# Batch 0's four head pairs merged in one written order on all engines

## The chip, the cores and the metric

One core of one Trainium2 chip runs the whole kernel as one program. The metric is device time in microseconds, as the median of several executions. The engines named here: TensorE (PE; its weight loads are listed as PEld), VectorE (DVE), ScalarE (ACT), GpSimd (POOL), and SyncE (SP), whose queue issues the DMA transfers.

## The reference

Attention in two parts, added, and a feed-forward layer on the result. The eight batches have eight heads, 576 positions and head dimension 64; the layer has 4608 tokens, width 512 and hidden width 2048.

```python
q_d, k_d, v_d = (mean over groups of 4 positions)      # 144 positions
out_up = np.repeat(softmax(scale * q_d @ k_d.T) @ v_d, 4, axis=2)
mask = np.abs(pos[:, None] - pos[None, :]) < 4         # a band of 7
out_local = softmax(where(mask, scale * q @ k.T, -1e9)) @ v
x = (out_up + out_local) as [batch * position, head * dim]
h = x @ w_in
out = (s * max(h, 0) ** 2 + b) @ w_out
```

## The kernel before, in words

**Units.** Attention is done for two heads at a time, a head pair (b, hp): 32 units. Units of batches 0 to 2 (`first_unit`) compute both parts on TensorE. The *far* part (`down`) sums q and k over four positions on VectorE (L276, L278), copies q into a block-diagonal tile on ScalarE (L282), sums v on GpSimd (L287 to L292), takes 3 score matmuls (`sa`, L303), the maximum (L304), three exponentials (L307), the normalisation (L311 to L314), transposes through TensorE (`tp`, `tr`, L322 to L327), copies them out (L329, L332) and multiplies with the summed v (`up`, L337, L339). The *near* part makes the banded scores from 24 small matmuls a head (`sl`, L388) on top of a mask matmul (L383), subtracts the maximum (L393, L394), takes the exponential (L397), normalises (L398 to L401, the last on GpSimd in batch 0), transposes in blocks of 32 on VectorE (L411), copies the blocks into a block-diagonal tile `bd` (L414) and multiplies with windows of v (`ol`, L431). L434 adds both parts into the tile x. Units of later batches do the near part on GpSimd and VectorE (`local_unit`).

**Rooms.** Unit (0,0) uses the standing tiles; units (0,1) to (0,3) borrow memory of weight tiles that are not filled yet (`make_room`), so that batch 0's units have no tile in common. Their block-diagonal tiles have to be zero first: `clear(i)` does that with GpSimd memsets (L187, L188). Unit (0,0)'s tiles `dq` and `db` are cleared by VectorE (L163, L174).

**Feed-forward.** Tokens go in 18 row blocks t of 256, the hidden width in 8 blocks p of 256. Each operand is split into a high and a low part and three products are taken: `gemm1(t, p)` (L556 to L558) into `ph`, activation on ScalarE (L566 to L568), low part on VectorE (`gl`, L569), `gemm2(t, p)` (L601 to L603). Weights arrive as 64-bit numbers and are rebuilt as 32-bit ones by `convert`: one ScalarE step (L226), four VectorE steps (L227 to L230), the high part on ScalarE (L231), the low part on VectorE (L234). Block p's raw words are staged in the memory of a later block's tile, `STAGE[p]`. `split_x(t)` splits the tokens (L542, L543).

**Order.** Row blocks 0 and 1 go through p = 0 to 6 together, then row block 2 does the same, then p = 7 for the three, then the others one by one. Weight block p is converted at a written step (`CONVERT_AT`), some with lowered priority (`BEHIND`). Batch 1 has to be complete before row block 2 starts. `advance` emits the steps of the attention units between the GEMMs at a written pace.

A scheduler reorders what the program emits: it keeps, for each engine, a list by priority (program order, moved by `high_priority`), and puts whichever instruction is ready first on the engine's queue by its own model of time. The queues are then fixed. Batch 0 is emitted unit by unit, with raised priority, so the scheduler decides how its units mix, and what else is put between:

```python
bk = banks(0, 1, 2, 3, 5, 6, 7)
for hp in range(HP):
    load_ahead(hp)
    if hp > 1:
        clear(hp)
    with tc.high_priority(offset=400):
        for _ in first_unit(0, hp, bk):
            pass
split_w(0)
```

PSUM has eight banks; batch 0's tiles take seven in turn, and bank 4 is left to the first `gemm1`.

Of the kernel before, what the change touches and what calls it, by code (L numbers as in the profile page):

```python
# [19 lines left out]
P = 128  # L20
# [29 lines left out]
STAGE = (6, 6, 7, 6, 7, 6, 7)  # L50
# [6 lines left out]
W_MAX = (1.875 - 2.0 ** -23) * 2.0 ** (31 - 127)  # L57

# [4 lines left out]
def attention_ffn_kernel(ctx, tc, qk, vw_in, vr_in, vdm, qkn, vn, w_in, w_out, s_in, b_in, out):  # L63
# [40 lines left out]
    def load_pair(b, hp):  # L104
        if (b, hp) in ld:
            return
        own = {}
        if b == 0 and hp:
            room[hp] = make_room(hp)
            own = room[hp]["load"]  # L110

        def load(tag, shape, src, pool=one):
            t = own[tag] if tag in own else pool.tile(shape, F32, tag=tag, name="t" + tag)
            nc.sync.dma_start(t, src)
            return t

        tqk = load("qk", [P, 2, SP], qk[b, hp], two)
        tvr = load("vr", [P, FAC, D], vr_in[b, hp])
        tvd = load("vd", [KM, FAC, P], vdm[b, hp])
        tvw = load("vw", [P, NG, P], vw_in[HP * b + hp]) if HP * b + hp < EU else None  # L120
        ld[(b, hp)] = (tqk, tvw, tvr, tvd)

    load_pair(0, 0)


    ident = cst.tile([P, P], F32, name="ident")
    make_identity(nc, ident)
    load_pair(0, 1)
# [25 lines left out]
    nc.gpsimd.memset(omask, 0.0)  # L154
    for u in range(2):
        mu = omask[64 * u : 64 * u + 64]
        keep(mu, [[1, CH], [1, NO]], -HALO, CH)
        keep(mu, [[-1, CH], [-1, NO]], S - 1 + HALO, -CH)

    dq = cst.tile([P, NQ * 2 * GQ + 3 * P], F32, name="dq")
    nc.vector.memset(dq, 0.0)  # L163
# [10 lines left out]
    nc.vector.memset(db, 0.0)  # L174
# [7 lines left out]

    def clear(i):
# [30 lines left out]
    def convert(st, hi, lo, op, p):  # L214
# [11 lines left out]
        nc.scalar.mul(f, top.bitcast(F32), 2.0 ** -112)  # L226
        nc.vector.tensor_scalar(f, f, W_MAX, -W_MAX, ALU.min, ALU.max)  # L227
        nc.vector.tensor_scalar(w, w, 3, 0x7FFFFFF8, ALU.logical_shift_left, ALU.bitwise_and)
        nc.vector.scalar_tensor_tensor(w, low, 29, w, ALU.logical_shift_right, ALU.bitwise_or)
        nc.vector.scalar_tensor_tensor(w, top, -0x80000000, w, ALU.bitwise_and, ALU.bitwise_or)  # L230
        nc.scalar.copy(hi, f)  # L231
        for i in range(0, n, 512):
# [3 lines left out]
    def split_w(p):  # L236
        with tc.high_priority(offset=-BEHIND.get(p, 0)):
            split_parts(p)

    def split_parts(p):  # L240
        wi[p] = one.tile([P, 2, NK, 256], F32R, tag=f"wi{p}", name="wi")
        wo[p] = one.tile([P, 2, 2, DM], F32R, tag=f"wo{p}", name="wo")
        for op, w in (("i", wi[p]), ("o", wo[p])):
            fl = w.rearrange("p s k f -> p s (k f)")
            if p < len(STAGE):
                st = wst.pop((p, op))
                for j in range(0, 1024, CHUNK[p]):
                    js = slice(j, j + CHUNK[p])
                    convert(st[:, js], fl[:, 0, js], fl[:, 1, js], op, p)
            else:  # L250
                for i in range(4):
                    cs = slice(256 * i, 256 * i + 256)
                    convert(load_quarter(p, op, i), fl[:, 0, cs], fl[:, 1, cs], op, p)
# [14 lines left out]
    def down(b, hp, banks, tmp, dg):  # L268

        _, qc, vdr, vm = dg  # L270
        tqk, _, tvr, tvd = ld[(b, hp)]
        qt, kt = tqk[:, 0], tqk[:, 1]

        qd = tmp([P, SD], "qd")
        kd = tmp([P, SD], "kd")
        nc.vector.tensor_reduce(  # L276
            qd, qt[:, 0:S].rearrange("p (s j) -> p s j", j=FAC), AX.X, ALU.add)
        nc.vector.tensor_reduce(  # L278
            kd, kt[:, 3 : 3 + S].rearrange("p (s j) -> p s j", j=FAC), AX.X, ALU.add)
        for h in range(2):  # L280
            hs = slice(64 * h, 64 * h + 64)
            nc.scalar.copy(  # L282
                qc[hs, :, GQ * h : GQ * h + GQ], qd[hs].rearrange("p (i s) -> p i s", i=NQ))
# [5 lines left out]
        for h in range(2):  # L289
            hs = slice(64 * h, 64 * h + 64)  # L290
            ve.tensor_tensor(vm[:, h, hs], vt[0:KM, 0, hs], vt[0:KM, 1, hs], ALU.add)
            ve.tensor_tensor(vdr[hs, hs], vq[hs, 0], vq[hs, 1], ALU.add)  # L292
        yield
# [7 lines left out]
        with first(b):  # L301
            for i in range(NQ):
                nc.tensor.matmul(sa[:, i], qc[:, i], kd, start=True, stop=True)  # L303
# [466 lines left out]
```

## Time and profile before

| | |
|---|---|
| median of 3 runs | 971.13 us (970.21 to 973.34) |
| span of the profiled execution | 970.7 us |
| TensorE busy | 938.7 us, 97% |
| VectorE busy | 637.7 us, 66% |
| ScalarE busy | 475.0 us, 49% |
| GpSimd busy | 418.0 us, 43% |
| DMA | 86.26 MB, mean 89 GB/s |

The profile is of one execution, and its span, 970.7 us, is 0.4 us under the median. Times in it are microseconds from the span's start. A row of the timeline gives start, duration, engine, line, operation, tiles and shapes, and in brackets how long the engine sat idle before and what ended that. A row of the groups gives, behind the bar, the busy time and the mean duration in ns, then the idle time before the group's instructions and its main releasers. Matmuls overlap and their ends are modelled, so their distances from start to start say more than their durations.

### The profile page before, as it was taken

The numbers are of one execution on the slowest core, as the hardware profiler recorded it, in microseconds if no ns is written. First come the engines' busy times: TensorE is split into PE (matmuls) and PEld (weight loads), VectorE is DVE, ScalarE is ACT, GpSimd is POOL, SyncE is SP. The second block draws the span as 40 slices with busy tenths as digits, with TensorE's granted clock in tenths as the row PEclk, the third lists the DMA queues.
The fourth block names the chain that finished last, engine by engine and source line by source line (L and its number), as shares of the span: only waits on it lengthen the run. The fifth ranks groups of instructions, "written<-read, shape, count | busy, mean of one in ns | idle before, by whom it ended". The sixth has DMA issues, their size and how long they took to land.

```text
span 970.7 us, 18541 instructions
## 1 busy us (share of the span) xinstructions
PE 938.7 (97%) x7316; PEld 843.4 (87%) x7316; DVE 637.7 (66%) x1175; ACT 475.0 (49%) x1141; POOL 418.0 (43%) x455
## 2 busy tenths in 40 slices
PE   5769999999999999999999999999999999999998
PEld 4559988888999999998888899989899999998987
DVE  5999996864567878787787878787878521211121
ACT  5878775553754453545363545453635433333231
POOL 9421011101066686776868786867676200000000
PEclk9999999999999999999999999999999999999999
DMA  9736512112243232323241424242412000000000
GB/s 316 261 121 210 172 60 78 49 42 73 101 134 113 77 110 72 102 70 133 67 136 66 135 68 131 72 134 69 136 55 76 1 22 1 23 1 22 1 23 22
DMA packets 32103, 86.26 MB, mean 89 GB/s; under 512 B 3344, under 2 KB 7952, under 8 KB 32016
## 3 DMA queue, kind: packets, MB, share of 16 engines
q1 hardware_dynamic: 32016, 85.08, 26.6%
q8 instruction: 57, 0.93, 0.4%
q14 instruction: 30, 0.25, 0.1%
HBM read 75.63 MB, written 9.44 MB: 88 GB/s over the span
## 4 chain that ended last, share of the span: by engine, by line
PE 74%; DVE 9%; DMA 8%; POOL 5%; ACT 2%; issue 2%; SPq 0%; DVEq 0%; ACTq 0%; POOLq 0%
PE ph L556 11%; PE ph L557 11%; PE ph L558 11%; PE po L603 11%; PE po L601 11%; PE po L602 11%; DMA tqk<-in_qk_dram 3%; POOL pr L466 3%; POOL acc L488 3%; DMA wst<-in_moe_w_out_dram 2%; PE sa L303 2%; DVE bias L579 1%; PE up L339 1%; PE ol L431 1%; DMA lqk<-in_qkn_dram 1%
## 5 line engine op out<-in xcount | busy, mean ns | idle before, releaser
L556 PE MATMUL ph<-xh,wi 128*128 128x256 f32 x1152 | 325.4, 283 | 3.7 <-ACT xh L542 2.5
L557 PE MATMUL ph<-xl,wi 128*128 128x256 f32 x1152 | 323.9, 281 | 0.0
L558 PE MATMUL ph<-xh,wi 128*128 128x256 f32 x1152 | 323.6, 281 | 0.0
L466 POOL TENSOR_TENSOR pr<-lqk 128x576 f32<-128x576 f32 x140 | 201.2, 1461 | 73.2 <-DMA lqk<-in_qkn_dram 29.2
L556 PEld LDWEIGHTS ph<-xh,wi 128*128 128x128 f32 x1152 | 217.5, 189 | 11.2 <-ACT xh L542 2.8
L557 PEld LDWEIGHTS ph<-xl,wi 128*128 128x128 f32 x1152 | 217.4, 189 | 5.4 <-issue 0.2
L558 PEld LDWEIGHTS ph<-xh,wi 128*128 128x128 f32 x1152 | 217.6, 189 | 0.3
L566 ACT ACTIVATE ph<-ph 128x512 f32<-128x512 f32 x144 | 83.8, 582 | 229.0 <-PE ph L558 223.2
L601 PE MATMUL po<-wo,gh 128*128 128x512 f32 x456 | 180.7, 396 | 0.0
L602 PE MATMUL po<-wo,gh 128*128 128x512 f32 x456 | 180.5, 396 | 0.0
L603 PE MATMUL po<-wo,gl 128*128 128x512 f32 x456 | 177.9, 397 | 0.0
L569 DVE TENSOR_TENSOR gl<-ph,gh 128x512 fp32r<-128x512 f32 x114 | 77.8, 683 | 115.8 <-ACT gh L568 115.5
L488 POOL TENSOR_TENSOR acc<-acc,pv 128x576 f32<-128x576 f32 x80 | 114.4, 1430 | 57.1 <-DVE acc L488 29.5
L468 DVE TENSOR_REDUCE st<-pr 128x9 f32<-128x576 f32 x140 | 105.9, 757 | 37.7 <-POOL pr L466 35.4
L292 POOL TENSOR_TENSOR dq<-vq 64x64 f32<-64x64 f32 x58 | 22.8, 393 | 197.4 <-PE up L337 195.3
L603 PEld LDWEIGHTS po<-wo,gl 128*128 128x128 f32 x456 | 85.7, 188 | 17.6 <-issue 0.2
L487 DVE TENSOR_TENSOR pv<-lv,st 128x576 f32<-128x576 f32 x120 | 87.5, 747 | 18.8 <-POOL acc L488 18.4
L601 PEld LDWEIGHTS po<-wo,gh 128*128 128x128 f32 x456 | 85.7, 188 | 15.9 <-ACT gh L568 0.6
L602 PEld LDWEIGHTS po<-wo,gh 128*128 128x128 f32 x456 | 85.7, 188 | 15.8
L568 ACT CAST gh<-ph 128x512 fp32r<-128x512 f32 x114 | 66.9, 587 | 64.3 <-PE po L602 62.4
L567 ACT ACTIVATE ph<-ph 128x512 f32<-128x512 f32 x144 | 83.7, 582 | 3.2
L602 PE MATMUL po<-wo,gb 128*128 128x512 f32 x120 | 47.1, 392 | 0.0
(149 smaller groups left out, 1239.3 us busy)
## 6 DMA issues: line engine op xcount, KB each, us to landing
tqk<-in_qk_dram SPq DMA_DIRECT2D x30, 584.0 KB, 4.1
lqk<-in_qkn_dram SPq DMA_DIRECT2D x20, 768.0 KB, 4.2
lv<-in_vn_dram SPq DMA_DIRECT2D x20, 480.0 KB, 3.4
out_dram<-os SPq DMA_DIRECT2D x17, 512.0 KB, 3.1
wst<-in_moe_w_in_dram SPq DMA_DIRECT2D x7, 1024.0 KB, 6.5
wst<-in_moe_w_out_dram SPq DMA_DIRECT2D x7, 1024.0 KB, 5.3
tvd<-in_vdm_dram SPq DMA_DIRECT2D x29, 160.0 KB, 2.9
tvr<-in_vr_dram SPq DMA_DIRECT2D x29, 128.0 KB, 3.1
```

Of the source, the lines that this page charges most:

```text
L466: nc.gpsimd.tensor_tensor(pr, lqk[:, 0:CH], lqk[:, CH + o : 2 * CH + o], ALU.mult)
L468: nc.vector.tensor_reduce(ls[:, :, o], pr, AX.X, ALU.add)
L487: nc.vector.tensor_tensor(pv, lv[:, o : o + CH], w, ALU.mult)
L488: (nc.vector if o % 3 == 1 else nc.gpsimd).tensor_tensor(acc[:, :, h], acc[:, :, h], pv, ALU.add)
L556: nc.tensor.matmul(ph[:, j], wi[p][:, 0, k, f], xh[:, k], start=(k == 0), stop=False)
L557: nc.tensor.matmul(ph[:, j], wi[p][:, 0, k, f], xl[:, k], start=False, stop=False)
L558: nc.tensor.matmul(ph[:, j], wi[p][:, 1, k, f], xh[:, k], start=False, stop=(k == NK - 1))
L566: nc.scalar.activation(ph, ph, AF.Relu)
L567: nc.scalar.activation(ph, ph, AF.Square)
L601: nc.tensor.matmul(po[m], gh[:, j, ms], wo[p][:, 0, j], start=first, stop=False)
L602: nc.tensor.matmul(po[m], gh[:, j, ms], wo[p][:, 1, j], start=False, stop=False)
L603: nc.tensor.matmul(po[m], gl[:, j, ms], wo[p][:, 0, j], start=False, stop=last)
```

## The change

Batch 0 is no longer emitted unit by unit. `first_unit` is taken apart into three step generators per unit: d (far part, 12 steps), l (near part, 13 steps) and v (value sums on GpSimd, one step). The conversion of weight block 0 becomes four more (c0 to c3, five steps each) and the split of row blocks 0 and 1 another (x, 8 steps; the first three pairs, then the fourth). A written string, `FRONT`, lists 132 steps in the order in which they are emitted, and `in_order` adds a dependency from each instruction to the one before it on its engine, so that the scheduler can't change this order. The first step of units (1,0) and (1,1) is chained behind it the same way.

The other edits: batch 0's PSUM tiles take all eight banks. The q/k tiles of the four pairs are loaded first, then all values, then the value windows of pair 0, weight block 0, and the windows of pairs 1 to 3; weight blocks 1 and 2 follow. Block 0 is staged in block 7's tiles instead of block 6's. Rooms 1 and 2 are cleared by ScalarE copies from a zero column, room 3 by VectorE memsets. The offset mask of the later batches is made after the front. Later units are emitted step by step as before.

```diff
-STAGE = (6, 6, 7, 6, 7, 6, 7)
+STAGE = (7, 6, 7, 6, 7, 6, 7)
...
+FRONT = (
+    "d0 l0 d0 d1 l1 d1 d0 d2 d1 d2 d0 l0 d0 v0 d2 d1 d0 d3 d1 l3 d2 v2 d1 d3 l1 l0 d2 d1 "
+    "l3 d0 l2 l0 d1 l3 d2 l2 l0 d0 l0 l2 d2 l0 c0 d2 d3 l2 v1 l3 l2 l3 d2 d3 c1 l2 d3 l1 "
+    "l0 l2 c0 d2 d1 v3 l1 d3 l0 c0 d0 d3 l2 d2 l3 c0 c1 d1 l0 c1 l1 d3 d1 l1 d0 c0 l1 l2 "
+    "d0 l3 l1 d3 d0 d2 l0 c2 c1 l2 c2 l1 l3 l0 l2 c1 l2 l0 d3 c2 l1 d1 c3 l2 l3 d3 l1 c3 "
+    "c3 l1 d3 l3 l1 x l3 x l3 x l3 c3 x c3 x c2 x x x c2 "
+)
...
-    load_pair(0, 0)
+    for hp in range(HP):
+        load_parts(0, hp, ("qk",))
+    for hp in range(HP):
+        load_parts(0, hp, ("vr", "vd"))
+    load_parts(0, 0, ("vw",))
...
     def clear(i):
         da, vm = room[i]["dg"], room[i]["sc"][:, 1536:1792]
         n = 2 * NG * P
-        for j in range(0, n + QV, 488):
-            nc.gpsimd.memset(da[:, j : min(j + 488, n + QV)], 0.0)
-        nc.gpsimd.memset(vm, 0.0)
+        for part in (da[:, n : n + QV], vm, da[:, 0:n]):
+            if i == 3:
+                nc.vector.memset(part, 0.0)
+            else:
+                nc.scalar.copy(part, zero.to_broadcast([P, part.shape[1]]))
...
+    def first_unit(b, hp, banks):
+
+        part = banded(b, hp, banks)
+        for steps in ("ddv", "ddd", "ll", "ll", "lll", "ddd", "ddll", "dd", "ll", "ll"):
+            with in_order() if steps == "ddv" and b == 1 and hp < 2 else contextlib.nullcontext():
+                for which in steps:
+                    next(part[which])
+            yield
...
+    @contextlib.contextmanager
+    def in_order():
+
+        traced = nc.cur_bb.bb.instructions
+        last = traced[-1]
+        yield
+        start = next(k for k in reversed(range(len(traced))) if traced[k] is last) + 1
+        for i in traced[start:]:
+            if i.engine in ENGINES:
+                if i.engine in tail:
+                    tc.add_manual_dep(
+                        i, tail[i.engine].name,
+                        mybir.DependencyInfo(
+                            mybir.DependencyClass.NoSync, mybir.DependencyReason.DATA),
+                        reason="in_order")
+                tail[i.engine] = i
+
+    def begin_x():
+        for t in range(2):
+            xs[t] = tuple(
+                two.tile([P, HP, TB], F32R, tag=tag, name=tag) for tag in ("xh", "xl"))
+        for hs in (slice(0, HP - 1), slice(HP - 1, HP)):
+            for t in range(2):
+                xh, xl = xs[t]
+                src = xt[0][:, hs, t * TB : t * TB + TB]
+                nc.scalar.copy(xh[:, hs], src)
+                yield
+                nc.vector.tensor_tensor(xl[:, hs], src, xh[:, hs].bitcast(F32), ALU.subtract)
+                yield
...
     load_w(0)
+    for hp in range(1, HP):
+        load_parts(0, hp, ("vw",))
...
-    bk = banks(0, 1, 2, 3, 5, 6, 7)
+    load_w(1)
+    bk = banks(0, 1, 2, 3, 4, 5, 6, 7)
+    with tc.high_priority(offset=400):
+        with in_order():
+            nc.vector.memset(dq, 0.0)
+            for hp in range(1, HP):
+                clear(hp)
+            nc.vector.memset(db, 0.0)
+    streams = {}
     for hp in range(HP):
-        load_ahead(hp)
-        if hp > 1:
-            clear(hp)
-        with tc.high_priority(offset=400):
-            for _ in first_unit(0, hp, bk):
-                pass
-    split_w(0)
-    load_w(1)
+        for name, steps in banded(0, hp, bk).items():
+            streams[f"{name}{hp}"] = steps
+    with tc.high_priority(offset=400):
+        with in_order():
+            chunks = split_parts(0)
+            streams["x"] = begin_x()
+            for name in FRONT.split():
+                if name not in streams:
+                    streams[name] = next(chunks)
+                next(streams[name], None)
+            next(chunks, None)
+    offset_mask()
+    load_pair(*units[HP])
+    load_pair(*units[HP + 1])
     load_w(2)
-    split_x(0)
-    split_x(1)
```

More of the change, by code (lines that the diff above doesn't have):

```diff
@@ L102, in make_room, with load_parts, load_pair @@
                 "sm": take(pl, at + 384, [P, 2, 2 * NG])}
[L104 to L108, printed above, removed]
-            room[hp] = make_room(hp)
-            own = room[hp]["load"]
-        def load(tag, shape, src, pool=one):
+    def load_parts(b, hp, parts):
+        if b == 0 and hp and hp not in room:
+            room[hp] = make_room(hp)
+        own = room[hp]["load"] if b == 0 and hp else {}
+        got = ld.setdefault((b, hp), {})
+        for tag in parts:
+            shape, src, pool = {
+                "qk": ([P, 2, SP], qk[b, hp], two),
+                "vr": ([P, FAC, D], vr_in[b, hp], one),
+                "vd": ([KM, FAC, P], vdm[b, hp], one),
+                "vw": ([P, NG, P], vw_in[min(HP * b + hp, EU - 1)], one)}[tag]
             t = own[tag] if tag in own else pool.tile(shape, F32, tag=tag, name="t" + tag)
             nc.sync.dma_start(t, src)
[L115 to L121, printed above, removed]
-    load_pair(0, 0)
+            got[tag] = t
+    def load_pair(b, hp):
+        if (b, hp) not in ld:
+            load_parts(b, hp, ("qk", "vr", "vd") + (("vw",) if HP * b + hp < EU else ()))
+    for hp in range(HP):
[3 more added lines that the diff above has]
+    load_parts(0, 0, ("vw",))
     ident = cst.tile([P, P], F32, name="ident")
     make_identity(nc, ident)
-    load_pair(0, 1)
     mask = cst.tile([P, 3, 32], F32, name="mask")
@@ L153, in attention_ffn_kernel, with offset_mask @@
     omask = cst.tile([P, CH, NO], F32, name="omask")
[L154 to L158, printed above, removed]
+    def offset_mask():
+        nc.gpsimd.memset(omask, 0.0)
+        for u in range(2):
+            mu = omask[64 * u : 64 * u + 64]
+            keep(mu, [[1, CH], [1, NO]], -HALO, CH)
+            keep(mu, [[-1, CH], [-1, NO]], S - 1 + HALO, -CH)
     dq = cst.tile([P, NQ * 2 * GQ + 3 * P], F32, name="dq")
-    nc.vector.memset(dq, 0.0)
     QV = NQ * 2 * GQ + P
@@ L237, in split_w @@
         with tc.high_priority(offset=-BEHIND.get(p, 0)):
[L238 removed]
+            for chunk in split_parts(p):
+                for _ in chunk:
+                    pass
     def split_parts(p):
@@ L266, in first, with add_values @@
         return tc.high_priority() if b >= 3 else contextlib.nullcontext()
[L268 to L283, printed above, removed]
+    def add_values(b, hp, tmp, dg):
+        _, _, vdr, vm = dg
+        tvr, tvd = ld[(b, hp)]["vr"], ld[(b, hp)]["vd"]
         vt = tmp([P, 2, P], "vt")
@@ L292, in down @@
             ve.tensor_tensor(vdr[hs, hs], vq[hs, 0], vq[hs, 1], ALU.add)
+    def down(b, hp, banks, tmp, dg):
+        _, qc, vdr, vm = dg
+        tqk = ld[(b, hp)]["qk"]
+        qt, kt = tqk[:, 0], tqk[:, 1]
+        qd = tmp([P, SD], "qd")
+        kd = tmp([P, SD], "kd")
+        nc.vector.tensor_reduce(
+            qd, qt[:, 0:S].rearrange("p (s j) -> p s j", j=FAC), AX.X, ALU.add)
+        nc.vector.tensor_reduce(
+            kd, kt[:, 3 : 3 + S].rearrange("p (s j) -> p s j", j=FAC), AX.X, ALU.add)
+        yield
+        for h in range(2):
+            hs = slice(64 * h, 64 * h + 64)
+            nc.scalar.copy(
+                qc[hs, :, GQ * h : GQ * h + GQ], qd[hs].rearrange("p (i s) -> p i s", i=NQ))
         yield
@@ new lines, in banded, with down_unit @@
+        return {"d": far(), "v": values(), "l": near()}
+    def first_unit(b, hp, banks):
[4 more added lines that the diff above has]
+                    next(part[which])
+            yield
+    def down_unit(b, hp, banks):
+        x = new_x(b)
+        tmp = lambda shape, name: one.tile(shape, F32, tag=name, name=name)
+        dn = down(b, hp, banks, tmp, diag[0])
@@ L411, in first_unit @@
-        nc.vector.transpose(pt, pl)
-        for w in range(4):
-            ws = slice(32 * w, 32 * w + 32)
-            nc.scalar.copy(bd[ws, :, ws], pt[ws])
-        yield
+        for count in (3, 3, 2):
+            for _ in range(count):
+                next(dn)
+            yield
         try:
```

160 lines of the change are left out of this document (90 added, 70 removed).

## The prediction

> **What bounds the kernel now.** I read the page's busy shares first, then a table of stretches, then the timeline of TensorE at the start.
>
> ```profile
> span 970.7 us, 18541 instructions
> PE 938.7 (97%) x7316; PEld 843.4 (87%) x7316; DVE 637.7 (66%) x1175; ACT 475.0 (49%) x1141; POOL 418.0 (43%) x455
> ```
>
> TensorE is busy in 97% of the span, so 32 us are left without it. The table of stretches (start and end, length, then busy time of each engine) says where:
>
> ```profile
> 0.00:5.00 5.00, 0.00 (x0) 0.00 (x0) 2.04 (x3) 1.28 (x1) 3.99 (x15) 1.00 0.63 187
> 5.00:30.00 25.00, 16.84 (x324) 13.51 (x324) 15.97 (x38) 15.32 (x53) 22.80 (x55) 1.00 1.04 355
> 30.00:51.00 21.00, 17.16 (x275) 14.08 (x265) 20.63 (x51) 18.12 (x52) 5.28 (x6) 1.00 0.60 199
> 51.00:69.20 18.20, 10.79 (x120) 8.64 (x116) 17.34 (x37) 13.83 (x30) 5.71 (x7) 1.00 0.38 122
> 69.20:140.40 71.20, 71.20 (x766) 64.07 (x764) 68.20 (x122) 54.74 (x118) 8.15 (x12) 1.00 0.45 150
> 140.40:157.00 16.60, 16.60 (x145) 14.89 (x135) 12.51 (x32) 10.36 (x23) 2.52 (x6) 1.00 0.36 116
> 157.00:270.00 113.00, 111.24 (x1121) 96.44 (x1120) 68.91 (x137) 58.62 (x147) 11.81 (x24) 1.00 0.19 63
> 270.00:970.70 700.70, 694.87 (x4607) 631.77 (x4606) 432.10 (x763) 302.75 (x721) 357.73 (x333) 1.00 0.22 72
> ```
>
> 24.4 of the 32 us lie before 69.2 us; behind it TensorE is full. What is to be seen besides is the third number, VectorE: from 30 to 140.4 us it is busy for 106.2 of 110.4 us. The kernel has two bounds in a row: TensorE from 69.2 us to the end, and VectorE from 30 to 140 us, which prepares what TensorE consumes. The timeline shows where the first GEMM starts, and how tight the two run at the last weight block that both start-up row blocks share (p = 6):
>
> ```profile
> 7.28 1.72 PE L303 MATMUL sa<-kd,dq 128*96 128x144 f32 x6 [7.28 <-DVE kd L278]
> 64.57 0.58 PE L556 MATMUL ph<-xh,wi 128*128 128x256 f32 x1 [2.50 <-ACT xh L542]
> 69.24 0.58 PE L557 MATMUL ph<-xl,wi 128*128 128x256 f32 x1
> 71.96 0.41 PE L557 MATMUL ph<-xl,wi 128*128 128x256 f32 x1
> 72.59 0.28 PE L557 MATMUL ph<-xl,wi 128*128 128x256 f32 x1
> 105.90 0.90 PE L303 MATMUL sa<-kd,dq 128*96 128x144 f32 x6
> 139.13 1.63 DVE L234 TENSOR_TENSOR wi<-es,wi 128x512 fp32r<-128x512 f32 x3 [1.24 <-ACT wi L231]
> 145.38 0.28 PE L556 MATMUL ph<-xh,wi 128*128 128x256 f32 x1
> ```
>
> One lone GEMM matmul runs at 64.57, then the stream starts at 69.24. The row at 139.13 holds the last low parts of w_in block 6 (done by 140.4) and one of block 7; TensorE reaches block 6 at 145.38. So the weights were ready 5.0 us ahead there. Much of the 20 us lead that VectorE had built before 69.2 us (block 1 converted, batch 1's first unit nearly done) has been used up.
>
> **The change, part by part.** *The merged front.* Batch 0's four head pairs no longer go one behind another with other work between; 132 steps (d: far path, l: near path, v: value sums, c: a 512-column weight chunk, x: split of x) are chained on each engine. Nothing of it may be overtaken by its own later steps, and the first step of units (1,0) and (1,1) is chained behind it. VectorE's work for that front, from the groups up to 69.3 us (busy, mean ns):
>
> ```profile
> L229 DVE SCALAR_TENSOR_TENSOR es<-wst,es 128x512 int32<-128x512 int32 x10 | 6.8, 675 | 0.0
> L230 DVE SCALAR_TENSOR_TENSOR es<-wst,es 128x512 int32<-128x512 int32 x10 | 6.6, 675 | 0.0
> L227 DVE TENSOR_SCALAR es<-es 128x512 f32<-128x512 f32 x10 | 4.8, 493 | 0.4 <-ACT es L226 0.4
> L228 DVE TENSOR_SCALAR es<-es 128x512 int32<-128x512 int32 x10 | 4.4, 440 | 0.0
> L276 DVE TENSOR_REDUCE qd<-tqk 128x144 f32<-128x576 f32 x4 | 3.0, 742 | 0.4 <-DMA tqk<-in_qk_dram 0.4
> L234 DVE TENSOR_TENSOR wo<-es,wo 128x512 fp32r<-128x512 f32 x4 | 2.7, 668 | 0.0
> L434 DVE TENSOR_TENSOR x<-ol,flat 128x288 f32<-128x288 f32 x6 | 2.6, 441 | 0.0
> L543 DVE TENSOR_TENSOR xl<-x,xh 128x1024 fp32r<-128x1024 f32 x2 | 2.4, 1208 | 0.0
> L394 DVE TENSOR_TENSOR flat<-sl,flat 128x192 f32<-128x192 f32 x6 | 2.0, 332 | 0.0
> L393 DVE TENSOR_REDUCE flat<-sl 128x6 f32<-128x192 f32 x6 | 1.9, 324 | 0.0
> L304 DVE TENSOR_REDUCE flat<-sa 96x3 f32<-96x432 f32 x3 | 1.8, 592 | 0.0
> L411 DVE STREAM_TRANSPOSE flat<-flat 128x384 f32<-128x384 f32 x3 | 1.7, 573 | 0.2 <-POOL flat L401 0.2
> L398 DVE TENSOR_REDUCE flat<-flat 128x12 f32<-128x384 f32 x3 | 1.6, 542 | 0.2 <-ACT flat L397 0.2
> L400 DVE RECIPROCAL flat<-flat 128x12 f32<-128x12 f32 x3 | 0.6, 211 | 0.0
> L174 DVE MEMSET db<- 128x1536 f32 x1 | 1.3, 1338 | 0.3 <-issue 0.3
> L163 DVE MEMSET dq<- 128x672 f32 x1 | 0.6, 618 | 0.9 <-PEq L758 0.9
> ```
>
> A pair: two big reductions 2 x 0.74, the maximum 0.59, two near halves 2 x (0.33 + 0.33), the sum 0.54, three small ones at about 0.2, the transpose 0.57, two additions 2 x 0.44: 6.0 us, four pairs 24.0. Four chunks at 0.675 + 0.675 + 0.49 + 0.44 + 0.67 = 2.95: 11.8. Two splits at 1.21: 2.4. The old clears 1.34 + 0.62, mask casts some 0.9. And the new part, room 3's clear: 1536 columns as db, 1.34, and 416 + 256 columns as dq, 0.62: 1.96 us added. Together 43.0.
>
> *Where the front ends.* TensorE did five units before 69.2 us, in 16.84 + 17.16 + 10.79 = 44.8 us busy: 9.0 each, 36 for four. It can start at 7.3, so without a stall its part ends at 43.3; then the last addition and the last quarter of two splits (0.44, and quarters of 1.05 and 1.21, twice, between other steps): 2.5, 46 us. VectorE alone gives 43 + 1 idle before its first memset + tail, about 45. No merged order of three engines at 70 to 80% runs without waits (in 30 to 51 us, the best stretch of before, TensorE still idled 18%); I take 10% and put the GEMM at 50 (46 to 55), VectorE's end at 51, with 43 us done and 8 idle. Before, it had done 38.6 by 51.0.
>
> *What follows.* Until the last w_in block is converted VectorE was busy 2.04 + 15.97 + 20.63 + 17.34 + 68.20 = 124.2 us; with room 3's clear 126.1. After: 126.1 - 43.0 = 83.1 left at 51 us, and idle as in before from 51 to 140.4 (0.86 + 3.00): 51 + 83.1 + 3.9 = 138.0, 2.4 us sooner than 140.4. TensorE now waits there instead of coming 5.0 us later, so block 6 starts 7.4 us sooner. A little can be put behind that point (of block 7 and of batch 1): I take 8. TensorE's own bound is wider: from 69.2 to 145.4 it worked 76.2 us, and unit (1,0), done in the idle front until now, falls into that stretch at some 5 us (9.0 x 0.90 / 1.72, by the six score matmuls here and there); 50 + 76.2 + 5 = 131.2, 14.2 sooner. So of the 19 us by which the GEMM starts sooner VectorE gives 8; behind block 6 TensorE is full again and keeps it.
>
> *ScalarE's clears* of rooms 1 and 2 are not in the trace. Nearest rows: copies of 512 and of 1024 columns,
>
> ```profile
> L231 ACT CAST wi<-es 128x512 fp32r<-128x512 f32 x5 | 3.1, 617 | 0.5 <-DVE es L230 0.3
> L542 ACT CAST xh<-x 128x1024 fp32r<-128x1024 f32 x2 | 2.1, 1046 | 1.7 <-DVE x L434 1.7
> L282 ACT COPY dq<-qd 64x144 f32<-64x144 f32 x6 | 1.8, 308 | 4.5 <-DVE qd L276 4.5
> ```
>
> 0.84 ns a column: 1536, 416 and 256 columns cost 1.47 + 0.54 + 0.40 = 2.4 a room, 4.8. ScalarE idled 4.5 us before its first copy, so about 1 us sticks out and delays qc, within the 10% above. Bounds: nothing, if they end before the first q; twice the price, if the broadcast source halves the rate, which moves the front 5 us and costs VectorE up to 5.
>
> *q and k first.* The four q/k transfers stand ahead of 1.6 MB of values. In 5 to 30 us the queues moved 355 GB/s, so 2.4 MB land by some 9 us. Values and block 0 come no later than before in bytes ahead of them; vw of pairs 1 to 3 moves behind block 0 (2.1 MB, 6 us), to about 22 us; the first step that needs one, pair 2's ol, is the 94th of 132, past 30 us: zero, hidden by the far and near paths. If it were late, TensorE would stop with all behind it, for as long as the landing is late.
>
> *POOL* loses the clears and postpones the offset mask: nothing on the path. *Bank 4* frees when pair 3's far result is copied, before the GEMM needs it: zero. *Staging block 0 apart from block 1* lets block 1 load early; VectorE has no time for it sooner: zero. The other units keep their order inside a step: zero.
>
> **The clock.** Up to the first GEMM matmuls TensorE works slowly: 0.41 us a matmul at 71.96, 0.28 at 72.59, and six score matmuls 1.72 against 0.90. It did so although it was busy for 17.16 of 21 us from 30 to 51, and the granted clock in the table reads 1.00 all the while. So the sum uses the slow prices for the whole front. [...]
>
> **Rivals.** (1) *TensorE is the bound, not VectorE*: the scheduler fills VectorE's 8 idle us of the front with block 1. Gain 12 to 14.2: 957 to 959. For it: before, VectorE's holes from 30 us on were filled. Against: the conversion's two buffers are held by the front's own four chunks, and batch 1 is chained behind it. (2) *TensorE turns fast inside the front*: its 36 us shrink towards 36 x 0.90 / 1.72 = 19, the GEMM starts with VectorE's 45 to 46, VectorE idles 4 us less, gain 12: 959. (3) *No change*: the front's waits are as long as the old ones (VectorE idle 16.2 us up to 140.4), and room 3's 1.96 us eat the rest, or the static order meets late data: 968 to 974. (4) *Slower, by batch 1's chain*:
>
> ```profile
> 36.16 0.73 DVE L276 TENSOR_REDUCE qd<-tqk 128x144 f32<-128x576 f32 x1
> L434 DVE TENSOR_TENSOR x<-ol,ups x8: 437/444/450, 70.7 to 155.4; 128x288 f32<-128x288 f32 x8
> ```
>
> Unit (1,0) began at 36.16 and its additions ended at 72, the fourth unit's at 155.9: 28 us a unit. Now nothing of batch 1 begins before 51. If 28 us were the units' own length, four end at 51 + 112 = 163, 7 us later than before: 978. It decides from (155.9 - 51) / 4 = 26 us a unit up. For it: a unit's temporaries have one buffer each, so units can hardly overlap. Against it: a unit's own work is 6 us on VectorE and 9 on TensorE at its slow pace, so most of the 28 is sharing VectorE with conversions.
>
> **How the numbers follow.** The profiled execution spans 970.7; the median of the runs is 971.1, 0.4 above. 970.7 - 8 + 0.4 = 963. Chances: forecast 0.44 (959 to 968), rival 1 0.15 (953 to 959, with the GEMM at 46), rival 2 0.08, no change 0.16, slower 0.17. 0.3% is 2.9 us, what the runs can tell. Faster 0.68, same 0.15, slower 0.17. The range holds all but the last: 953 to 974.
>
> **What would show it.** Right: the stream of GEMM matmuls starts at 46 to 55; TensorE, full before, has waits of 1 to 3 us for VectorE's low parts between there and block 6; block 6 starts near 137; from 270 us on nothing is changed but the offset. Wrong: a front past 58 (ScalarE's clears or late vw named as releaser), TensorE without waits up to block 6 (rival 1), matmuls of 0.28 us from the first of the stream on (rival 2), or row block 2 waiting for batch 1's last x (rival 4).

## The result, and the profile after

The changed kernel is slower: 981.55 us (median of 4 runs, 979.86 to 985.12) against 972.24 us for the kernel before on the same chip, a ratio of 1.0099 (95% interval 1.0075 to 1.0124). Forecast were 963 and a range of 953 to 974. The profiled execution is the one of 979.86 us, with a span of 978.1; against the 970.7 quoted before, 7.4 us more.

The page's head after:

```profile
span 978.1 us, 18539 instructions
PE 936.9 (96%) x7316; PEld 842.8 (86%) x7316; DVE 643.7 (66%) x1180; ACT 479.0 (49%) x1149; POOL 405.5 (41%) x440
```

TensorE does the same 7316 matmuls in 936.9 us, 1.8 less than before. So the whole loss is idle time of TensorE: 978.1 - 936.9 = 41.2 us against 970.7 - 938.7 = 32.0. Where it lies is seen when both spans are cut at the start of the GEMM stream and at 260 us. The kernel before (start and end, length, busy time of TensorE, its weight loads, VectorE, ScalarE, GpSimd, then granted clock, DMA share, GB/s):

```profile
0.00:69.20 69.20, 44.79 (x701) 36.23 (x701) 55.98 (x126) 48.55 (x135) 37.78 (x81) 1.00 0.70 234
69.20:260.00 190.80, 189.04 (x1939) 166.93 (x1938) 145.10 (x278) 117.33 (x272) 20.66 (x36) 1.00 0.31 103
260.00:970.70 710.70, 704.87 (x4680) 640.24 (x4678) 436.62 (x772) 309.14 (x736) 359.55 (x338) 1.00 0.22 71
```

The changed kernel, and below the two cuts again in finer stretches:

```profile
0.00:48.30 48.30, 30.29 (x610) 26.10 (x610) 39.75 (x87) 38.81 (x107) 24.67 (x60) 0.81 0.79 269
48.30:260.00 211.70, 193.60 (x1860) 167.90 (x1853) 160.56 (x312) 124.88 (x290) 19.50 (x36) 0.94 0.31 102
260.00:978.10 718.10, 712.99 (x4857) 648.83 (x4855) 443.34 (x782) 315.27 (x754) 361.32 (x344) 1.00 0.22 72
...
140.40:153.90 13.50, 13.50 (x136) 11.20 (x134) 7.41 (x18) 6.29 (x15) 2.20 (x5) 1.00 0.36 110
153.90:171.00 17.10, 7.63 (x92) 6.29 (x92) 10.99 (x30) 9.65 (x29) 2.79 (x6) 0.57 0.27 85
171.00:270.00 99.00, 95.77 (x1015) 83.42 (x1014) 58.84 (x112) 48.92 (x124) 8.13 (x18) 0.99 0.21 68
```

Length less TensorE's busy time is its idle time. Ahead of the GEMM 24.41 us have become 18.01, a gain of 6.4. From there to 260 us 1.76 have become 18.10, a loss of 16.3, and 9.47 of them lie in one stretch, 153.9 to 171.0. Behind 260 us nothing has changed (5.83 and 5.11). The 20.9 us by which the GEMM starts sooner are thus 6.4 us of removed waits; the other 14.5 are TensorE work that no longer lies ahead of the start, most of which comes back behind it.

The stretch at 153.9 is a wait for batch 1. TensorE's timeline there, and the last instructions of VectorE that it waits for:

```profile
157.45 0.32 PE L421 MATMUL sl<-maskb,idb 128*128 128x192 bf16 x1 [3.55 <-ACT pd L335]
161.55 0.82 PE L368 MATMUL up<-ptr,dq 128*128 128x144 f32 x2 [1.32 <-issue]
165.96 2.19 PE L464 MATMUL ol<-db,tvw 128*64 128x96 f32 x24 [2.64 <-ACT db L454]
169.64 1.75 PE L329 MATMUL sa<-kd,dq 128*96 128x144 f32 x6 [1.49 <-DVE x L468]
171.01 0.59 PE L613 MATMUL ph<-xh,wi 128*128 128x256 f32 x1
...
51.98 0.74 DVE L310 TENSOR_REDUCE qd<-tqk 128x144 f32<-128x576 f32 x1
169.83 0.45 DVE L468 TENSOR_TENSOR x<-ol,ups 128x288 f32<-128x288 f32 x1
170.48 0.96 DVE L600 TENSOR_TENSOR xl<-x,xh 128x768 fp32r<-128x768 f32 x1 [0.20 <-ACT xh L599]
```

Unit (1,0) begins at 51.98 (before: 36.16) and the fourth unit's last addition is at 169.83 (before, by the row of L434: 155.4). Only then can the tokens of row block 2 be split (170.48), and its first GEMM matmul stands at 171.01. No GEMM matmul runs meanwhile (none writes `ph` or `po` from 153.9 to 171.0): what TensorE does there are the small matmuls of the chain itself, each after a hop over ScalarE or VectorE, and at 169.64 the first ones of batch 2. The list of TensorE's waits says the same. From 69.2 to 260 us before:

```profile
PE sl L383 <- DVE pl L394: 1.1, 1, 1.1
PE sl L383 <- ACT pd L307: 0.5, 1, 0.5
PE ph L556 <- DVE gl L569: 0.2, 1, 0.2
```

and from 48.3 to 200 us after (total, count, longest):

```profile
PE sl L421 <- ACT pd L335: 3.5, 1, 3.5
PE ol L464 <- ACT db L454: 2.6, 1, 2.6
PE po L658 <- ACT wo L248: 2.3, 1, 2.3
PE sa L329 <- DVE x L468: 1.5, 1, 1.5
```

Why the hops are long, the chain of waits shows between 146 and 168 us:

```profile
146.09 2.83 DMA wst<-in_moe_w_in_dram
149.01 0.44 ACT es L240
150.13 0.43 DVE es L245
150.56 0.73 DVE x L468 x2
151.29 0.34 DVE es L246
151.68 2.58 DMA wst<-in_moe_w_out_dram
154.35 0.44 ACT es L240
155.35 0.61 DVE dmx L331
156.22 1.19 ACT pd L335 x6
...
164.73 2.86 DMA wst<-in_moe_w_out_dram
167.67 0.44 ACT es L240
```

Between batch 1's steps stand conversions of weight block 7, whose quarters (L240) are still being transferred. The 2.83, 2.58 and 2.86 us are the parts of three transfers that lie on the chain; ScalarE itself sits idle for 2.06, 2.29 and 1.76 us ahead of the three L240. The chain's next step runs only behind that conversion: on ScalarE at 154.68 (the copy of q), on VectorE at 150.56 and 169.21 (the additions).

### The profile page after: what moved, and what is told of

It is laid out like the page before. It is cut to its first block, busy times and chain, and to the rows that moved or that the text cites. A ratio compares the mean times of both kernels' runs of the same rounds, so it can differ in the third digit from the quotient of the medians.

```text
span 978.1 us, 18539 instructions
## 1 busy us (share of the span) xinstructions
PE 936.9 (96%) x7316; PEld 842.8 (86%) x7316; DVE 643.7 (66%) x1180; ACT 479.0 (49%) x1149; POOL 405.5 (41%) x440
## 4 chain that ended last, share of the span: by engine, by line
PE 74%; DVE 12%; POOL 4%; DMA 3%; ACT 3%; issue 3%; DVEq 0%; SPq 0%; POOLq 0%; ACTq 0%
PE ph L613 11%; PE ph L615 11%; PE ph L614 11%; PE po L658 11%; PE po L659 11%; PE po L660 11%; PE sa L329 2%; POOL acc L545 2%; POOL pr L523 2%; DVE es L245 1%; DVE es L246 1%; DMA wst<-in_moe_w_out_dram 1%; DMA wst<-in_moe_w_in_dram 1%; PE up L370 1%; DMA tqk<-in_qk_dram 1%
## 5 line engine op out<-in xcount | busy, mean ns | idle before, releaser
L623 ACT ACTIVATE ph<-ph 128x512 f32<-128x512 f32 x144 | 83.8, 582 | 231.5 <-PE ph L615 229.1
L300 POOL TENSOR_TENSOR dq<-vq 64x64 f32<-64x64 f32 x58 | 20.8, 358 | 194.0 <-PE up L368 191.9
L624 ACT ACTIVATE ph<-ph 128x512 f32<-128x512 f32 x144 | 83.8, 582 | 3.2
```

The source lines that it names most:

```text
L623: nc.scalar.activation(ph, ph, AF.Relu)
L624: nc.scalar.activation(ph, ph, AF.Square)
```

## The experiments

In the expectations theory 1 is that batch 1's four units are one serial chain, that it starts later behind the merged front, and that row block 2 waits for its end. Theory 2 is that VectorE's amount of work holds the stretch. Other rivals are told in each. Every ratio is against the kernel before on the same chip. "Idle" is TensorE's, the span less its busy time, in the profiled execution.

**No wait for batch 1 (gate_off).** `split_x(2)` takes its second piece from batch 0:

```diff
-            while (b, HP - 1) not in complete:
+            other = t == 2 and b == 1
+            while (b, HP - 1) not in complete and not other:
...
+            src = xt[0][:, :, 0:n] if other else xt[b][:, :, t0 - b * S : t0 - b * S + n]
```

> The changed kernel, but row block 2 takes its second piece of tokens from batch 0 instead of batch 1, so it waits for no unit of batch 1 (this leaves the right tokens out; the work is the same). Theory 1, batch 1's units are a serial chain that now starts behind the front, and row block 2 waits for its end: TensorE goes on at about 153 us instead of 171, saves the slow matmuls behind that wait too, 961 to 967 us. Theory 2, VectorE's throughput holds everything between 52 and 150 us and row block 2 only meets it: TensorE then waits for low parts of weights or of gh instead, gain under 6 us, 975 or more.

977.68 us, 1.0059 (1.0044 to 1.0074): some 4 us better than the changed kernel, far from the 961 to 967 of theory 1 and inside the range of theory 2. Idle is 40.6 us, hardly less than 41.2, and has moved:

```profile
PE up L368 <- issue: 3.4, 1, 3.4
PE po L659 <- ACT gh L626: 2.2, 2, 1.1
PE ph L614 <- DVE os L671: 1.9, 1, 1.9
PE po L659 <- DVE os L671: 1.7, 1, 1.7
```

These are waits between 140 and 262 us. Batch 1's last addition now ends at 175.6, and its matmuls still run between those of the GEMM: the wait of 3.4 us is ahead of such a matmul, at 166.33, though row block 2 no longer needs its result. The other three lie behind 214 us and name `gh` and `os`, not batch 1's tiles. Why they came up isn't shown.

**The same in the kernel before (gate_off_before).** 

> The kernel before with row block 2's second piece taken from batch 0's x, so that it does not wait for batch 1 (that part of the tokens is wrong in the output), the pair of gate_off. TensorE idles 1.8 us in 157 to 270 us in the kernel before, so the wait costs it little: 968 to 973 (theory 1: the gate is where the two kernels differ, and only the changed one loses there). If the gate also costs the kernel before (rival), 960 to 967.

974.45 us, 1.0028 (1.0017 to 1.0039). The wait costs the kernel before nothing; taking it away is even a little slower. The rival falls.

**Batch 1 on three PSUM banks (banks3).**

```diff
-    rings = {1: banks(5, 6), 2: banks(5), ...
+    rings = {1: banks(5, 6, 7), 2: banks(5), ...
-        ph = bank(... 7 if t == 1 and p < HF else 4, ...)
+        ph = bank(... 4, ...)
```

> The changed kernel, with three PSUM banks in turn (5, 6, 7) for batch 1's units instead of two (5, 6); row block 1's first products share bank 4 with row block 0's. Theory 1 in its narrow form, a unit's eight PSUM tiles through two banks make the chain serial: the units overlap, batch 1 is complete before row block 2 is due, 960 to 968 us, less what the shared bank 4 costs (14 pairs at 0 to 1 us). Theory 2, VectorE's throughput: the units take as long as before, 976 to 982.

985.78 us, 1.0139 (1.0122 to 1.0156). Both forecasts missed. The chain is shorter, its last addition ends at 156.1 instead of 170.3. But both row blocks now share one bank for `ph`, and TensorE pays for that:

```profile
PE po L658 <- ACT gh L625: 7.1, 5, 2.4
PE ph L613 <- DVE gl L626: 3.3, 2, 2.9
```

With a third bank a unit takes (156.1 - 52.2) / 4 = 26.0 us instead of 29.6, so the two banks are part of what sets the units' pace; the run can't show what a shorter chain is worth.

**Without the tie of units (1,0) and (1,1) (no_tie).** `in_order` around their first steps is left out. 

> The changed kernel, without the dependency that chains the first step of units (1,0) and (1,1) behind the front. Theory 3, this tie alone delays batch 1: row block 2 starts 10 us or more sooner, 965 to 972 us. Theory 1: batch 1's scores need a place behind the front's on TensorE and on ScalarE anyway, so the chain begins 0 to 4 us sooner, 977 to 982.

982.35 us, 1.0114 (1.009 to 1.0137), no different from the changed kernel. Unit (1,0) has its first VectorE step at 33.8 now, sooner than in the kernel before (36.2), its score matmuls at 49.2 (tied 55.0, before 43.3), and ends at 83.8 instead of 89.4; the fourth ends at 171.9. The written tie isn't the cause, and an early first step alone does not bring the end of the chain forward.

**Batch 1 late in the kernel before (late_before).** One dependency: the first step of (1,0) comes behind the splits of row blocks 0 and 1.

```diff
+        if (b, hp) == (1, 0):
+            for i in traced[start:]:
+                if i.engine in front_end:
+                    tc.add_manual_dep(i, front_end[i.engine].name, ...)
```

> The kernel before, with one thing added: the first step of unit (1,0) is chained behind the split of row blocks 0 and 1 on VectorE and ScalarE, so batch 1 starts at about 69 us instead of 36. Theory 1: four units at 25 to 30 us each end near 180 instead of 156, row block 2 waits 15 to 22 us, 985 to 995 us. Theory 2: VectorE fills its queue with conversions that it has to do anyway and loses nothing, 971 to 977.

987.9 us, 1.0174 (1.0152 to 1.0197), as theory 1 said. The GEMM stream starts at 63.8, 5 us sooner than before, because (1,0) is out of its way; the last addition is at 176.0, and the stretch ahead of row block 2 looks as in the changed kernel (23.0 us with 13.86 busy):

```profile
L444 DVE TENSOR_TENSOR x<-ol,ups x8: 447/449/452, 98.9 to 176.0; 128x288 f32<-128x288 f32 x8
...
157.00:180.00 23.00, 13.86 (x166) 11.18 (x165) 17.20 (x42) 11.72 (x37) 2.81 (x6) 0.68 0.26 92
```

The late start of batch 1 alone, with nothing of the merged front, costs 16 us.

**Less VectorE work, in both kernels (light, light_before).**

```diff
+        if p < 2:
             nc.vector.scalar_tensor_tensor(w, low, 29, w, ...)
             nc.vector.scalar_tensor_tensor(w, top, -0x80000000, w, ...)
```

> The changed kernel, with the two bit operations that put sign and low bits into a weight (0.67 us a chunk each) left out for blocks 2 to 7; VectorE has some 27 us less to do between 65 and 150 us, nothing else is touched. Theory 2, each of the nine or so VectorE steps of a batch 1 unit waits behind conversions, and that makes a unit 30 us long instead of 18: units of about 20 us, batch 1 complete before 145, no wait before row block 2, 958 to 968 us. Theory 1, the two PSUM banks and the late start make the chain: units of 27 us or more, row block 2 still after 160, 974 to 980 us.

> The kernel before with the two combining steps of a conversion left out for weight blocks 2 to 7 (some 27 us of VectorE up to row block 2), the pair of light. If VectorE's conversions set how long a unit of batch 1 takes (theory 1), its units take 24 us or less here too, batch 1 is complete by 145 us, and the time is 958 to 966, so that light (974.4) stays 8 to 16 us slower than its pair. If the chain's length comes from its own hops (rival), nothing changes before the gate: 968 to 973, and the pair's difference is 1 to 6 us.

The changed kernel comes to 974.41 us, 1.0030 (1.0014 to 1.0047): 7 of its 9 us are gone, in the range that theory 1 gave, and batch 1 ends at 159.8. The kernel before stays at 971.41, 1.0008 (0.9991 to 1.0025), though batch 1 ends at 152.5. Its stretch behind the start of the GEMM, with VectorE's 145.1 us down to 117.5 and TensorE's busy time the same to 0.1 us:

```profile
69.40:260.00 190.60, 189.14 (x1939) 166.94 (x1938) 117.47 (x236) 115.09 (x270) 17.29 (x36) 1.00 0.30 103
```

My expectation of 958 to 966 missed: behind the start of the GEMM VectorE was no bound of the kernel before. (The conversions of blocks 0 and 1, ahead of it, were left as they are.) In the changed one its load lengthens the chain.

**Low parts of weights on GpSimd (pool_lo, pool_lo_before).** `lo = f - hi` of blocks 1 to 6 by GpSimd. 

> The changed kernel, with the low parts of weight blocks 1 to 6 (0.67 us a chunk of 512 on VectorE) made by GpSimd, which is busy for a tenth of that stretch. VectorE has 13 us less to do from 52 to 150 us. Theory 2: units of 25 us, row block 2 some 10 us sooner, 966 to 974 us, if GpSimd's slower low parts (some 1.3 us a chunk) come in time. Theory 1: 977 to 983 us.

> The same edit in the kernel before, where TensorE has no wait between 69 and 160 us: both theories expect 969 to 973 us, no change. More than 4 us of gain would say that VectorE held the old kernel too.

981.84 us (1.0105, 1.0078 to 1.0133) and 988.43 us (1.0186, 1.0159 to 1.0213). The changed kernel doesn't move; the kernel before gets slower, which I had not expected: its GEMM starts at 72.5 and TensorE idles 31.5 us ahead of it instead of 24.4. The edit touches the order that the scheduler picks in the front. Nor did it take the work off VectorE as meant: the changed kernel has 24 VectorE instructions fewer, but VectorE's busy time stays at 644.2 us (643.7), because others of unchanged shape got longer, the step at L245 on 512 columns from 725 to 1034 ns and on 1024 columns from 1211 to 1860 (48 to 160 us). So the pair decides nothing.

**Clears by GpSimd in the changed kernel (clear_pool).**

```diff
-            if i == 3:
-                nc.vector.memset(part, 0.0)
-            else:
-                nc.scalar.copy(part, zero.to_broadcast([P, part.shape[1]]))
+            nc.gpsimd.memset(part, 0.0)
```

> The changed kernel, with all three rooms cleared by GpSimd as before, so VectorE has 1.96 us and ScalarE 4.8 us less at the start, and GpSimd some 6.6 us more, ahead of the value sums. If the clears cost the front something, the GEMM starts 1 to 3 us sooner than 48.3; if GpSimd's value sums are what the far results wait for, it starts 3 to 6 us later. Theory 1 and 2 alike leave row block 2 and the time within 3 us of the changed kernel.

A single run, without an interval: 993.27 us, not within the 3 us that either theory gave. Batch 0's last addition ends at 54.9 instead of 48.5, the GEMM starts at 54.7, batch 1 ends at 178.7. In the merged order the clears on ScalarE and VectorE are worth 6 us of the front and, in this one run, 12 us of time; that the 12 come by way of the chain is inferred from its later end.

**The same clears in the kernel before (before_clear).** The copies for room 2 read their source column after unit (0,0) has written there, so that room gets those values in place of zeros; the instructions and their sizes are the same. 

> The kernel before with one edit: rooms 1 to 3 cleared by ScalarE copies and VectorE memsets in place of GpSimd memsets. GpSimd was busy for 22.80 of the 25 us from 5 to 30, so if it sets when units (0,2) and (0,3) start, the front ends 2 to 5 us sooner and the time is 966 to 970; if TensorE and VectorE set the front by themselves, no change, 970 to 974. In the changed kernel the same clears were worth 12 us (993.3 with GpSimd).

978.49 us, 1.0060 (1.0040 to 1.0080). Single GEMM matmuls run from 61.3 on, the stream starts at 65.1, 4 us sooner, unit (1,0) ends at 72.5 as before (72.1), and still the fourth unit ends at 163.5 (before 155.9). Both forecasts missed: the chain got longer behind a sooner GEMM even though its first unit ended as before. Why, this run doesn't show.

**Row blocks 0 and 1 get their last weight block ahead of row block 2 (fill7, fill7_before).** To give TensorE something to do in the wait:

```diff
-    order = [(t, p) for p in range(HF) for t in range(2)]
-    order += [(2, p) for p in range(HF)]
-    order += [(t, p) for p in range(HF, NFP) for t in range(3)]
+    order = [(t, p) for p in range(NFP) for t in range(2)]
+    order += [(2, p) for p in range(NFP)]
...
-        if 2 * HF - 1 <= st < 2 * HF - 1 + NFP:
-            add_rows((NFP - 1, *range(NFP - 1))[st - 2 * HF + 1])
+        if 9 <= st < 9 + NFP:
+            add_rows(st - 9)
```

> The changed kernel, with weight block 7 of row blocks 0 and 1 put ahead of row block 2 (about 11 us of matmuls that do not need batch 1), and the sums of the weights' rows moved ahead accordingly. Theory 1, what costs the time is TensorE's wait for batch 1 before row block 2 (12 us of idle from 146 to 190 us and the slow matmuls behind it): the matmuls fill it, 967 to 973 us. Theory 2, VectorE's work is what holds this stretch: the wait goes to the low parts of block 7, 978 to 985 us.

> The order of fill7 in the kernel before, where TensorE has no wait before row block 2. Both theories: 968 to 974 us, no change; below that, block 7's place would be worth something by itself.

987.82 us (1.0153, 1.0138 to 1.0169) and 995.48 us (1.0239, 1.0222 to 1.0257): worse in both, and outside every forecast. Block 7 must now be ready sooner, and with it come the row sums of the weights on VectorE, some 21 us; batch 1 ends at 174.3, and TensorE waits at other places (6.2 us once for the block-diagonal tile `db`), 46.3 us in all. In the kernel before the front became longer too (30.0 us idle).

**Block 1's conversion left out (w1_free).** Block 0's tiles stand for block 1's. 

> The changed kernel, with block 1's conversion left out (its products use block 0's weights): VectorE has 11.4 us and ScalarE 5 us less to do right behind the front. If that conversion, which the old kernel did inside its front, is what takes TensorE's lead from 21 us to 13 between 57 and 80 us, the lead at the second block stays above 17 us. Theory 1: batch 1's chain still begins at 52 and takes 28 to 30 us a unit, row block 2 at 164 or later, 974 to 980 us. Theory 2: the units gain what VectorE gains, row block 2 at about 158, 967 to 973 us.

970.22 us, 0.9978 (0.9963 to 0.9993): 11 to 12 us better than the changed kernel, below the range of theory 1 and inside that of theory 2. With 9.8 us of VectorE work less (643.7 to 633.9), the fourth unit ends at 161.2. TensorE's idle time is 35.4 us instead of 41.2, and its busy time 931.3 instead of 936.9: here its GEMM matmuls take 0.28 us from 45.73 on. The lead (by how much sooner than in the kernel before the same amount of GEMM work is done) stays at 22 to 25 us until the wait begins; in the changed kernel it falls from 23 us at 55 us to 10 at 90 and is 13 at 140. So with block 1's conversion behind the front some 10 us of lead are lost, part of them to slower matmuls (on the `ph` tile 0.41 us at 69.26, 0.58 at 78.59 and 0.41 at 79.40, against 0.28 at 71.25). Behind the wait the lead is 0 to 4 us here and -6 to -11 in the changed kernel: where TensorE goes on is set by the end of batch 1, which comes sooner with less for VectorE and ScalarE to do.

**Block 7's conversion with lower priority (w7_late).** `BEHIND` gets `7: 400`. 

> The changed kernel, with block 7's conversion at the lowered priority of block 1. From 144 to 170 us ScalarE waits 2 to 4 us at a time for a quarter of block 7 to land, and batch 1's last unit stands behind it in the queue. Theory 1: the last unit's 18 us shorten by 2 to 5, 976 to 980 us. If the scheduler puts these conversions at the same places, nothing changes, 980 to 983.

980.61 us, 1.0082 (1.0065 to 1.0099), 1 us or nothing. The priority doesn't change ScalarE's order in this stretch: from 142 to 171 us it has the same instructions in the same order, with idle times of 1.88, 2.24 and 1.21 us ahead of L240.

**No batch 1 at all, in both kernels (no_b1, no_b1_before).**

```diff
-        for i in range(HP, EU):
+        for i in range(2 * HP, EU):
...
+    NY[1] = 0
+    complete.add((1, HP - 1))
...
-            src = xt[b][:, :, t0 - b * S : t0 - b * S + n]
+            src = xt[0 if b == 1 else b][:, :, t0 - b * S : t0 - b * S + n]
```

> The changed kernel without batch 1's four units: they are left out, and row blocks 2 to 4 take batch 0's x in their place. Its pair is no_b1_before; the difference of the two counts, not the distance to the kernel before. If batch 1's chain is what eats the lead (theory 1): the lead at the first row blocks is kept, the changed kernel is 10 to 16 us faster than its pair, and TensorE has under 4 us of idle time between 60 and 200 us. If the loss is VectorE's work pushed behind the front (rival): the lead shrinks at block 1 and up to block 6, and 0 to 5 us are left of it.

> The kernel before without batch 1's four units (left out as in no_b1). The GEMM stream starts at 60 to 66 us in place of 69, because unit (1,0)'s 9 us of TensorE are gone from the front. Time by theory 1 10 to 16 us above no_b1, by the rival 0 to 5 us above it. Against the kernel before 15 to 25 us faster, the four units' TensorE time.

947.5 us (0.9744, 0.9721 to 0.9767) and 955.17 us (0.9816, 0.9792 to 0.9840). The sign turns: without batch 1's units the same change makes the kernel 7.7 us faster, and the intervals are apart. The stretches of the changed one and of its pair, cut at the start of the GEMM stream:

```profile
0.00:50.63 50.63, 33.61 (x568) 28.96 (x568) 40.78 (x90) 39.41 (x108) 24.56 (x60) 0.76 0.78 257
50.63:260.00 209.37, 200.76 (x1687) 175.33 (x1688) 153.61 (x281) 118.48 (x256) 21.11 (x31) 0.98 0.28 92
```

```profile
0.00:65.18 65.18, 37.97 (x665) 30.86 (x666) 51.71 (x116) 44.77 (x125) 32.59 (x75) 0.73 0.71 236
65.18:260.00 194.82, 190.30 (x1541) 167.81 (x1542) 135.37 (x244) 108.00 (x226) 15.32 (x26) 0.98 0.26 87
```

Idle ahead of the GEMM is 17.0 against 27.2, behind it to 260 us 8.6 against 4.5. The gain of the front stays, less some waits. It is under the 10 to 16 that I gave theory 1, and over the 0 to 5 of the rival; the idle time from 60 to 200 us is 5.4 us, not under 4. Part of the rival is to be seen too: the lead over the pair is 13 us at 70 us, 9 at 90, and 4 to 7 from 130 on (lead as explained under w1_free).

**All edits but the merged order (unmerged).** Batch 0's units are emitted one by one, and the scheduler mixes them:

```diff
-            for name in FRONT.split():
-                ...
+    for hp in range(HP):
+        with tc.high_priority(offset=400):
+            for _ in first_unit(0, hp, bk):
+                pass
+    split_w(0)
...
+    split_x(0)
+    split_x(1)
```

> The changed kernel with batch 0's units emitted one by one again (the scheduler mixes them, as before), with all other edits: eight banks, q and k first, rooms cleared by ScalarE and VectorE, block 0 staged in block 7's tiles, offset mask after the front. If only the merged order does harm (by pushing batch 1 behind the front): unit (1,0) ends before 80 us again, and the time is 966 to 973. If an edit beside it does the harm: 976 to 982, as the changed kernel.

980.37 us, 1.0068 (1.0042 to 1.0093); the profiled execution is its lowest, 976.1. It came out as the second of the two forecasts: the edits beside the merged order do nearly the same by themselves.

```profile
L468 DVE TENSOR_TENSOR x<-ol,ups x10: 422/448/457, 38.0 to 167.2; 128x288 f32<-128x288 f32 x10
L468 DVE TENSOR_TENSOR x<-ol,flat x6: 445/448/457, 42.9 to 50.3; 128x288 f32<-128x288 f32 x6
```

Batch 0's last addition starts at 50.3 (merged 48.0, before 65.4), the GEMM stream at 55.8, and batch 1 ends at 167.7; its first unit begins at 35.2, as early as before, but ends at 80.5 instead of 72.1. TensorE's lead in GEMM work, 13 us ahead of the wait, is -6 behind it. So the written order itself is worth 2.3 us of batch 0's end and 7.5 us of the GEMM's start; the other edits together make the rest.

Start of the GEMM stream (from where its matmuls follow one another; single ones can come sooner) and TensorE's idle time, worked out from the profiled executions, side by side:

| kernel | GEMM starts | idle ahead | idle from there to 260 us | idle in all | batch 1 ends |
|---|---|---|---|---|---|
| before | 69.2 | 24.4 | 1.8 | 32.0 | 155.9 |
| light_before | 69.4 | 26.6 | 1.5 | 33.6 | 152.5 |
| before_clear | 65.1 | 24.0 | 5.4 | 35.5 | 163.5 |
| late_before | 63.8 | 26.6 | 11.2 | 42.9 | 176.5 |
| unmerged | 55.8 | 20.5 | 11.7 | 36.9 | 167.7 |
| after | 48.3 | 18.0 | 18.1 | 41.2 | 170.3 |
| no_b1_before | 65.2 | 27.2 | 4.5 | 37.5 | none |
| no_b1 | 50.6 | 17.0 | 8.6 | 30.7 | none |

Of all these versions none that does all of the work is faster than the kernel before.

## Why the prediction was wrong, point by point

**The front: right.** The GEMM stream was put at 50 (46 to 55):

```profile
43.10 1.21 PE L464 MATMUL ol<-flat 128*64 128x96 f32 x24 [1.54 <-ACT flat L454]
44.26 0.38 PE L613 MATMUL ph<-xh,wi 128*128 128x256 f32 x1
47.28 0.32 PE L421 MATMUL sl<-maskb,idb 128*128 128x192 bf16 x1 [2.64 <-DVE x L468]
48.32 0.58 PE L614 MATMUL ph<-xl,wi 128*128 128x256 f32 x1
50.88 0.28 PE L613 MATMUL ph<-xh,wi 128*128 128x256 f32 x1
```

It starts at 48.32. VectorE was to end at 51 with 8 us idle; by 48.3 it had worked 39.75 and idled 8.55. The clears came out as summed (0.40, 0.54 and 1.47 us a piece, by the row below), and ended at 6.35, beside the first q copy at 6.26, so not even the 1 us stuck out.

```profile
L202 ACT COPY flat<-dq x6: 398/534/1464, 2.0 to 4.9; 128x416 f32<-128x416 f32 x2, 128x256 f32<-128x256 f32 x2, 128x1536 f32<-128x1536 f32 x2
```

**Block 6 sooner by 8: near.** Its first matmul (the 289th of GEMM1) stands at 134.17, 11.2 us sooner than 145.38. But VectorE did not hold it back as forecast: of TensorE's 5.4 us of idle time from 48.3 to 140.4 us no wait names a low part of w_in. The waits named are for a high part of w_out (2.3 us), for `gl` (1.2) and for steps of a unit (0.9 and 0.7), and VectorE's low parts up to block 6 were done by 134.5, not 138.0. That the number is near is in part luck.

**"VectorE bounds from 30 to 140": wrong.** With 27.6 us of VectorE's work taken out of that part, the kernel before did not get faster (light_before). From 69.2 us on TensorE was full, and the busy VectorE only filled its time with work that was not yet needed. The row read rightly was the other one: weights ready 5.0 us ahead. For 30 to 69.2 us no run tested it.

**"Behind block 6 TensorE is full again and keeps it": the step that failed.** It is full until 153.9, and then idles 9.47 of 17.10 us. The forecast followed the weights to block 6 and not batch 1's chain to row block 2. Rival 4 had just that: nothing of batch 1 before 51 (measured 51.98), 28 us a unit (measured (170.3 - 52.0) / 4 = 29.6), end at 163 (170.3), 978 us (981.6). It was held against it that most of the 28 us is sharing VectorE with conversions. That the units share VectorE is so (with less of its work, in light, they take (159.8 - 51) / 4, some 27 us, and in w1_free (161.2 - 49.4) / 4, 28 us), but the sharing stays: the units meet the conversions behind the front, block 1's among them, which the kernel before had done inside it. The chance of 0.17 was too low, and the bar of 26 us a unit was passed by the only measurement there was.

**A lead counted as a gain.** The sums (8, 12 to 14) counted how much sooner a point of the GEMM is reached. While TensorE's busy time stays, what the end can gain is only the idle time that goes: its busy sum is 938.7, 936.9, 937.3 and 938.5 us in before, after, light_before and light (931.3 in w1_free is the lowest). The front had 24.4 us idle and kept 18.0. Without the chain the change gave 7.7; the 957 to 959 of rivals 1 and 2 was, by that measure, not to be had with this front.

**Rival 2, TensorE fast inside the front: seen in part.** The 24 matmuls of `ol` take 1.21 us at 43.10, behind a wait of 1.54 us, and 2.19 at 165.96, behind one of 2.64. All four units' work on TensorE, put at 36 us at the slow price, came to 28.8 (560 matmuls up to 44.2 us). Behind the 24 matmuls TensorE waits 2.64 us, and the first GEMM matmuls are slow again (0.58) until 50.88 (0.28). In no_b1 and w1_free the stream has matmuls of 0.28 us from its second on. Between the `ol` matmuls and the slow rows TensorE idles only those 2.64 us; what makes the rows slow no run shows. The stall at row block 2 is followed by the same: 0.59 us for the first matmul at 171.01, and 0.28 again at 173.56.

**What stays open.** Shown is that with batch 1's units the change loses 9 us and without them it gains 7.7 (no_b1 and its pair), and that a late start of batch 1 alone costs the kernel before 16 (late_before). Leaving the units out also takes work off VectorE, 20 us in the kernel before and 23 in the changed one; but light_before and light take off more, 25.6 and 30.6 us, and there the changed kernel is still not the faster one (light 1.0030, light_before 1.0008, the intervals overlap). So the loss hangs on the units and not on VectorE's amount of work alone. How it divides between the later start, the longer hops behind ScalarE's waits for transfers, and the conversions that now lie beside the chain is not settled: gate_off moved the waits, banks3 bought new ones, in no_tie, unmerged and before_clear the first step came early and the end of the chain late all the same, and w1_free won back 11 to 12 us by one conversion less. A version with ScalarE's waits for block 7 taken away by an earlier transfer wasn't tried.

## What to carry to other kernels

Where one engine is full, count its idle time, not the point at which a stage starts: work moved from ahead of a start to behind it is no gain, and unless the work itself gets faster, the most that a shorter front can give is the idle time in it. Follow every chain that ran in the shadow of the part that is compressed to its next deadline; here one that began 16 us later ended 14 us later, and what it feeds waited. An early first step is not enough: the chain ends late, too, when the work that the front no longer holds lands beside it. To see whether a busy second engine is a bound, take work out of it in the kernel as it is, before forecasting from its sum.

## What the runs showed of the hardware

The granted clock in the front differs between executions that do nearly the same work: 1.00 in the kernel before, 0.91 in light_before (a GEMM start of 69.2 and 69.4), 0.81 after, 1.00 in unmerged. In these four neither the start nor the time follows it. In the wait at 153.9 to 171.0 it reads 0.57, with TensorE busy for 7.63 of 17.10 us.

In the run in which GpSimd made the low parts of the weights (pool_lo), VectorE's step at L245 took 1034 and 1860 ns on 512 and 1024 columns, and 725 and 1211 ns in the changed kernel, where VectorE makes them itself. Why it took longer is not shown.
